# Linear attention with a one-token FFN on one core: kv sums in blocks of four token tiles, FFN batches of eight, part of wo on POOL's queue

## The chip, the cores and the metric

The kernel runs on one core of a Trainium2 chip. The metric is the device time of one execution in microseconds (us), the median over several executions. The profile covers a span that ends about 1.5 us short of that time. A run counts as fast unless it is over 1.5% above the fastest of the same kernel; every timed run told here is a fast one, except one single look whose state is not known.

## The reference, cut to what matters

```python
x = A_x                                              # 1 x 2048 x 1024, bf16
g = sigmoid((x * gate_w).sum(-1, keepdims=True))
# branch A: linear attention, 32 heads of 32, phi(t) = (t+1 if t>0 else exp(t)) + 1e-6
q, k, v = split(x @ wqkv)
kv = einsum("bhsd,bhse->bhde", phi(k), v);  z = phi(k).sum over s
o  = (phi(q) @ kv) / (phi(q) . z + 1e-6)
a  = o @ wo
# branch B: one FFN row, for the token with the largest x @ w_r, added at that row of x
y  = (silu(x_sel @ w_gate) * (x_sel @ w_up)) @ w_down * sigmoid(r_sel)     # F = 3584
b  = x with y added in that row
out = g * a + (1 - g) * b
```

## The kernel before

Names in the profile: `ps` is a buffer in PSUM, into which the program has TensorE write its results and out of which VectorE and ScalarE copy them ("evacuate" them); `pk` and `pq_all` are phi of k and q, `vt` is v, `kvacc` the kv sums, `wt` a streamed piece of weights, `h_bf` and `hps` h before and after its transposition, `yacc` and `yps` the down projection before and after its last sum, and `xp` a copy of x into which the chosen row, with y added, is written.

TensorE multiplies 16 token tiles by wk and wv (`unit_KV`, four units of eight 128x512 matmuls per tile), with units of q (`unit_Q`) between. Into this stream of full 128*128 matmuls two other kinds are mixed. The kv sums use 128*64 tiles:

```python
def unit_KVACC(t):
    for g in range(NG):
        for h in range(2):
            pe.matmul(kv_slot(g)[64 * h : 64 * h + 64, :], lhsT=pk_t[t][:, g * P + 64 * h : g * P + 64 * h + 64],
                      rhs=vt_t[t][:, g, h, :], start=False, stop=False, skip_group_check=True, tile_position=(0, 64 * h))
    # ... (the two buffers are given back)
```

The FFN of the one chosen row uses 128*32 tiles, four column tiles at a time; its weights stream through nine buffers, one piece after another:

```python
for j in range(4):        # compute() of one piece of gate_up
    pe.matmul(ps[32 * j : 32 * j + 32, 0:w], lhsT=xs_pad[:, c, :], rhs=wt[:, w * j : w * j + w],
                     start=(c == 0), stop=(c == KC - 1), tile_position=(0, 32 * j))
# ... after the last piece of up: h on VectorE, and h_transpose is left "pending" for ffn_flush()
```

The down projection is not on TensorE: VectorE adds each row of w_down, scaled by h, to `yacc`. What is mixed where is decided by tables and by this loop:

```python
GU_AFTER = {(6, "end"), (7, 1), (7, "end"), (8, 1), (8, "end"), (9, "end"), (10, "end"), (11, "end")}
# ...
def ffn_step(n):
    for _ in range(n):
        ffn_flush()
        wt, comp = inflight.popleft()
        comp(wt)
        ffn_prefetch()
# ...
for t in range(4, NT):
    for nb in range(4):
        unit_KV(t, nb)
        if nb == 1 and t > 4 and t % 2 == 0:
            unit_KVACC(t - 2)
            unit_KVACC(t - 1)
        if (t, nb) in GU_AFTER:
            ffn_step(4)
        steps = DOWN_STEPS.get(t, ())
        if nb < len(steps):
            down_step(steps[nb])          # also flushes first
    # ... units of q, FFN batches at the "end" of a token tile
```

After that come the denominators (`dps`), the product of kv with wo (`pm`), the rest of q, and 16 output tiles of 16 matmuls each.

## Time and profile before

| | before |
|---|---|
| time, median | 254.4 us (254.27 to 254.54, 3 runs) |
| span of the profile | 252.7 us |
| visits of 128*64 and 128*32 tiles from token tile 4 on | 6 kv blocks of 32 matmuls, 8 FFN batches of 16, one pair of them adjacent |
| last matmul start to end of the span | 248.59 to 252.72: 4.1 us |

How long SyncE (SP) closes the program shows in the view of the kernel's last line, restricted to SP. Columns: operation, count, duration ns min/median/max, first and last start us.

```profile
L702 SPq EVENT_SEMAPHORE  x12: 17/28/28, 249.9 to 252.7; - x12
L702 SPq DRAIN  x3: 7/7/128, 251.7 to 252.2; - x3
```

SyncE starts its closing checks (waits for the semaphores of queues and engines) at 249.9, and reaches its first drain at 251.7, 1.8 us on. The first drain takes 128 ns.

### The profile page before, as it was taken

The page shows a single profiled execution, that of the slowest core. Times are in us where ns is not written, and L with a number is a line of the kernel's source. Part 1 is how long each engine was busy: PE and PEld are TensorE (multiplying, and loading weights), DVE is VectorE, ACT ScalarE, POOL GpSimd, SP SyncE. Part 2 cuts the span into 40 slices and gives each one's busy share as a digit, 9 for nine tenths or more (in the row PEclk, how much of TensorE's full clock was granted, in tenths as well). Part 3 has the DMA queues.
Part 4 walks back from the last instruction along what each step waited for, and adds up shares of the span by engine and source line. Part 5 has one row for each costly group of instructions (what it writes and reads, how often), then busy time and mean ns, then how long its engine had stood idle before and what let it go on. Part 6 is the DMA issues. An engine that isn't in the chain of part 4 may idle for free.

```text
span 252.7 us, 4218 instructions
## 1 busy us (share of the span) xinstructions
PE 246.5 (98%) x1626; PEld 110.6 (44%) x1626; DVE 146.4 (58%) x240; ACT 125.4 (50%) x200; POOL 47.6 (19%) x94
## 2 busy tenths in 40 slices
PE   7999999999999999999999999999999999999993
PEld 2444454444444444444444444444444444444442
DVE  0045024324164369996899712585888999954442
ACT  2096334545354445555545635568888633333300
POOL 5000011010000000000000000210666689940000
PEclk9999999999999999999999999999999999999999
DMA  6999990029999989869896860030000573454122
GB/s 212 292 335 225 255 338 11 0 67 324 350 349 334 341 269 313 291 199 333 292 488 219 199 137 0 17 127 9 0 1 5 161 221 136 165 168 159 49 83 84
DMA packets 47499, 47.74 MB, mean 189 GB/s; under 512 B 18732, under 2 KB 35380, under 8 KB 47416
## 3 DMA queue, kind: packets, MB, share of 16 engines
q1 hardware_dynamic: 47192, 47.34, 61.5%
q8 instruction: 12, 0.20, 0.3%
q0 software_dynamic: 256, 0.14, 0.2%
q14 instruction: 7, 0.06, 0.1%
q10 hardware_dynamic: 32, 0.00, 0.0%
HBM read 39.34 MB, written 8.40 MB: 189 GB/s over the span
## 4 chain that ended last, share of the span: by engine, by line
PE 95%; DMA 2%; SPq 0%; DVE 0%; issue 0%; DVEq 0%
PE ps L78 88%; PE first L78 3%; PE kvacc L78 2%; DMA wkv<-in_A_wqkv_dram 2%; PE dps L78 1%; PE rps L78 1%; PE pm L78 1%; SPq L78 0%; DVE ot L78 0%; PE yps L78 0%; PE xs_ps L78 0%; DVEq L702 0%; PE pt L78 0%; PE hps L78 0%; PE wps L78 0%
## 5 line engine op out<-in xcount | busy, mean ns | idle before, releaser
L78 PE MATMUL ps<-wkv,xT 128*128 128x512 bf16 x480 | 107.3, 379 | 0.0
L78 PEld LDWEIGHTS <-xT 128*128 128x128 bf16 x512 | 48.6, 98 | 60.2 <-issue 3.7
L78 PE MATMUL ps<-xT,wq 128*128 128x512 bf16 x256 | 58.4, 379 | 0.0
L78 PE MATMUL ps<-m_sb,pq_all 128*128 128x512 bf16 (+2 forms) x264 | 55.6, 373 | 0.0
L78 ACT ACTIVATE u<-ps 128x512 f32<-128x512 f32 x60 | 35.8, 597 | 39.6 <-PE ps L78 38.0
L78 ACT ACTIVATE e<-u 128x512 f32<-128x512 f32 x64 | 40.3, 630 | 2.0
L605 POOL TENSOR_TENSOR pq_all<-pq_all,rb 128x512 bf16<-128x512 bf16 x32 | 36.6, 1168 | 14.4 <-DVE rb L78 13.9
L78 PEld LDWEIGHTS <-pq_all 128*128 128x128 bf16 x264 | 25.5, 98 | 30.2 <-issue 0.4
L78 PEld LDWEIGHTS <-wq 128*128 128x128 bf16 x256 | 24.5, 98 | 30.4 <-issue 1.7
L78 DVE SCALAR_TENSOR_TENSOR pq_all<-ps,e 128x512 bf16<-128x512 f32 x32 | 22.0, 688 | 26.2 <-ACT e L78 26.0
L78 DVE SCALAR_TENSOR_TENSOR yacc<-wt,hcol,yacc 128x1024 f32<-128x1024 bf16 x27 | 34.6, 1280 | 2.8 <-DMA wt<-in_B_w_down_dram 2.2
L78 ACT CAST vt<-ps 128x512 bf16<-128x512 f32 x32 | 18.8, 587 | 33.2 <-PE ps L78 33.2
L78 DVE SCALAR_TENSOR_TENSOR ot<-ps,gate,xg 128x512 bf16<-128x512 f32 (+2 forms) x33 | 23.8, 733 | 15.1 <-PE ps L78 14.2
L78 ACT ACTIVATE xg<-xt,omg 128x1024 f32<-128x1024 bf16 x16 | 18.1, 1145 | 25.9 <-DVE ot L78 25.9
L78 DVE SCALAR_TENSOR_TENSOR pk<-ps,e 128x512 bf16<-128x512 f32 x28 | 19.2, 686 | 18.3 <-ACT e L78 18.3
L78 DVE STREAM_SHUFFLE rb<-rdp 128x512 f32<-128x512 f32 x32 | 22.7, 742 | 0.0
L205 POOL MEMSET vt<- 128x16 bf16 x16 | 2.5, 191 | 105.5 <-PE kvacc L78 105.0
L78 DVE CAST r_bf<-rps 128x512 bf16<-128x512 f32 x1 | 0.7, 692 | 12.6 <-PE rps L78 12.6
L78 PE MATMUL first<-wkv,xT 128*128 128x512 bf16 x32 | 7.2, 379 | 0.7 <-DMA wkv<-in_A_wqkv_dram 0.6
L78 DVE SCALAR_TENSOR_TENSOR pk<-first,e 128x512 bf16<-128x512 f32 x4 | 2.8, 691 | 8.6 <-ACT e L78 8.6
L78 PE MATMUL ps<-wt,xs_pad 128*32 128x512 bf16 (+1 forms) x128 | 7.5, 355 | 0.0
L514 POOL DMA_DIRECT2D xp<-brow x1 | 0.6, 573 | 34.3 <-DVE zcol L78 34.3
(96 smaller groups left out, 82.7 us busy)
## 6 DMA issues: line engine op xcount, KB each, us to landing
wt<-in_B_w_down_dram SPq DMA_DIRECT2D x14, 512.0 KB, 6.2
wt<-in_B_w_gate_dram SPq DMA_DIRECT2D x8, 512.0 KB, 6.9
wt<-in_B_w_up_dram SPq DMA_DIRECT2D x8, 512.0 KB, 8.8
xt<-xp SPq DMA_DIRECT2D x16, 256.0 KB, 2.9
out_dram<-ot SPq DMA_DIRECT2D x15, 256.0 KB, 2.0
wt<-in_B_w_gate_dram SPq DMA_DIRECT2D x8, 384.0 KB, 5.9
wt<-in_B_w_up_dram SPq DMA_DIRECT2D x8, 384.0 KB, 6.9
wkv<-in_A_wqkv_dram SPq DMA_DIRECT2D x8, 256.0 KB, 5.1
```

The lines of the kernel that those rows point to most:

```text
L78: inst = fn(*a, **k)
L205: nc.gpsimd.memset(vt_t[t][:, :, :, 64:65], 1.0)
L514: nc.gpsimd.dma_start(out=xp[bass.ds(nonlocal_idx[0], 1), :].rearrange("o (j n) -> (o j) n", j=4), in_=brow[0:128:32, :])
L605: nc.gpsimd.tensor_tensor(sl, sl, rb[:], op=ALU.mult)
```

## The change

The intent is fewer changes of TensorE's tile shape: kv sums four token tiles at a time, the second FFN half in two batches of eight pieces, and two FFN batches placed right behind a kv block. The rest makes room for that: a fifth kv buffer, another order of weight pieces and down steps, transpositions of h at fixed later places in place of "before the next step", and eight of the 16 wo loads on POOL's queue.

```diff
-GU_AFTER = {(6, "end"), (7, 1), (7, "end"), (8, 1), (8, "end"), (9, "end"), (10, "end"), (11, "end")}
+GU_AFTER = {(6, "end"): 4, (7, 1): 4, (7, "end"): 4, (8, 1): 4, (10, 1): 8, (12, 1): 8}
+FLUSH_AFTER = {(8, 3), (13, 0)}
 ... (DOWN_STEPS: 28 steps as before, placed later)
-    kvp = ph1.enter_context(tc.tile_pool(name="kvp", bufs=4))
+    kvp = ph1.enter_context(tc.tile_pool(name="kvp", bufs=5))
 ... (wo_pieces)
-                    ld = nc.sync.dma_start(out=wt[32 * r : 32 * r + 32, :].rearrange("p (c n) -> p c n", c=2),
-                                           in_=wo_v[k // 2, r][:, 2 * (k % 2) : 2 * (k % 2) + 2, :])
+                    eng = nc.sync if r % 2 == 0 else nc.gpsimd
+                    ld = eng.dma_start(out=wt[32 * r : 32 * r + 32, :].rearrange("p (c n) -> p c n", c=2),
+                                       in_=wo_v[k // 2, r][:, 2 * (k % 2) : 2 * (k % 2) + 2, :])
 ... (ffn_pieces)
-        for _ in range(4):
-            yield from islice(gu, 4)
-            yield from islice(dn, 2)
+        for n in (2, 4):
+            yield from islice(dn, n)
+            yield from islice(gu, 8)
 ... (ffn_step, down_step)
-            ffn_flush()
 ... (token loop)
-            if nb == 1 and t > 4 and t % 2 == 0:
-                unit_KVACC(t - 2)
-                unit_KVACC(t - 1)
-            if (t, nb) in GU_AFTER:
-                ffn_step(4)
+            if nb == 1 and t > 4 and t % 4 == 0:
+                for t0 in range(t - 4, t):
+                    unit_KVACC(t0)
+            ffn_step(GU_AFTER.get((t, nb), 0))
+            if (t, nb) in FLUSH_AFTER:
+                ffn_flush()
 ...
-    unit_KVACC(NT - 2)
-    unit_KVACC(NT - 1)
+    for t in range(NT - 4, NT):
+        unit_KVACC(t)
```

More of the change, by code (lines that the diff above doesn't have):

```diff
@@ L33 @@
 Q_PER_T = {4: 2, 5: 1, 6: 1, 7: 2, 8: 1, 9: 1, 10: 2, 11: 1, 12: 1, 13: 1, 14: 1, 15: 0}
-GU_AFTER = {(6, "end"), (7, 1), (7, "end"), (8, 1), (8, "end"), (9, "end"), (10, "end"), (11, "end")}
+GU_AFTER = {(6, "end"): 4, (7, 1): 4, (7, "end"): 4, (8, 1): 4, (10, 1): 8, (12, 1): 8}
+FLUSH_AFTER = {(8, 3), (13, 0)}
 M_AFTER = {3: (0, 0), 6: (0, 1), 9: (1, 0), 12: (1, 1)}
-DOWN_STEPS = {9: (1, 1, 1, 1), 10: (1, 1, 1, 1), 11: (1, 1, 1, 1), 12: (1, 1, 1, 1, 1), 13: (1, 1, 1, 1), 14: (1, 1, 1, 1), 15: (1, 1, 1)}
+DOWN_STEPS = {9: (1, 1, 1, 1), 10: (0, 0, 1, 1, 1, 1), 11: (1, 1, 1, 1), 12: (0, 0, 1, 1, 1), 13: (1, 1, 1, 1, 1), 14: (1, 1, 1, 1, 1), 15: (1, 1, 1)}
 FFN_DEPTH = 9
@@ L496, in down_step @@
         for _ in range(n):
-            ffn_flush()
             if down["cur"] is None:
@@ L539 @@
             router_part2()
-        if (t, "end") in GU_AFTER:
-            ffn_step(4)
+        ffn_step(GU_AFTER.get((t, "end"), 0))
     unit_Q(*q_units.popleft())
-    unit_KVACC(NT - 2)
-    unit_KVACC(NT - 1)
+    for t in range(NT - 4, NT):
+        unit_KVACC(t)
     down_finish()
```

## The prediction

> **What bounds the kernel now.** I began with the page: busy shares first, then the chain that ended last.
>
> ```profile
> PE 246.5 (98%) x1626; PEld 110.6 (44%) x1626; DVE 146.4 (58%) x240; ACT 125.4 (50%) x200; POOL 47.6 (19%) x94
> ...
> PE 95%; DMA 2%; SPq 0%; DVE 0%; issue 0%; DVEq 0%
> ```
>
> TensorE (PE) is busy 98% of the span and is 95% of the chain, so only PE time moves the end. A busy PE need not be an efficient PE: matmul ends are modelled, so I read starts. Next I took the timeline of PE in the stretch where the attention stream (128*128 tiles) is interrupted by the FFN (128*32 tiles) and by the kv sums (128*64 tiles). Columns: start us, length, engine, line, operation, out<-in, tile, shape, count.
>
> ```profile
> 60.54 0.70 PE L78 MATMUL kvacc<-vt,pk 128*64 128x65 bf16 x32
> 61.17 3.63 PE L78 MATMUL ps<-wkv,xT 128*128 128x512 bf16 x16
> 64.63 1.89 PE L78 MATMUL ps<-xT,wq 128*128 128x512 bf16 x8
> 66.45 1.05 PE L78 MATMUL ps<-wt,xs_pad 128*32 128x512 bf16 x16
> 67.43 3.63 PE L78 MATMUL ps<-wkv,xT 128*128 128x512 bf16 x16
> 70.99 1.05 PE L78 MATMUL ps<-wt,xs_pad 128*32 128x512 bf16 x16
> 71.97 3.63 PE L78 MATMUL ps<-wkv,xT 128*128 128x512 bf16 x16
> 75.43 3.62 PE L78 MATMUL ps<-xT,wq 128*128 128x512 bf16 x16
> ```
>
> Read start to start. From 61.17 to 64.63, with no border behind them, 16 matmuls take 3.46 us, 0.216 each. The 16 from 67.43 to 70.99, with a border behind, take 3.56 us, 0.10 more. No wait shows there; PE never sits idle for a releaser in this stretch. The extra lies at the borders. Between single starts in the trace the last 128*128 matmul before a border is 0.309 us from its successor (0.093 too much), the last 128*32 one is 0.312 us from its successor (0.096 too much), and the first matmul after each border takes 0.227 (0.011 too much). These are costs of changing tile shape, and PE being "busy" hides them.
>
> Third, the chain in order of time shows what a kv block costs by its length:
>
> ```profile
> 36.50 1.14 PE kvacc L78 x64
> ...
> 60.61 0.63 PE kvacc L78 x32
> ```
>
> Another 32 matmuls cost 1.14 - 0.63 = 0.51 us, 16 ns each, so a block of 32 holds 0.63 - 0.51 = 0.12 us that does not depend on its length.
>
> **What the Trainium skill says.** "TensorEngine Tiling (Array Packing)", Key Properties: "Changing tiling mode (not just tile) drains the TensorE". The trace agrees; it puts about 0.10 us on each border. "TensorE: Matmul & The Clock Gate", Back-to-back issue gap, gives N/2.4 + 2.5 ns for a warm matmul: 216 ns at 512 columns, 162.5 at 384; the trace shows 216, and 162 between groups of four of 384 columns. It says four column tiles run together (Part 3); here four start within 10 ns of each other. "DMA: Bandwidth & Descriptors", Issuing engines are not separate DMA queues, says that spreading issues over engines saves only sequencer time. I rest on that for the wo part; no row here tests it.
>
> **The change part by part.** An excursion is a departure from the 128*128 stream and the return.
> - kv block, fixed cost: entry 0.093, inside 0.12, first matmul after it 0.011: 0.223 us.
> - FFN batch of 16 matmuls at 512 columns: 0.98 us first start to first start after it; its four groups at 0.216 make 0.864, leaving 0.116; with 0.093 and 0.011, 0.220 us.
>
> *kv sums in fours.* From token tile 4 on there are six blocks of 32 now and three of 64 after. The matmuls are the same, three excursions go: 3 x 0.223 = 0.67 us.
>
> *Second FFN half in two batches.* Four batches of 16 become two of 32: 2 x 0.220 = 0.44 us. Gate and up keep their eight groups of four.
>
> *FFN right behind kv blocks.* Now one FFN batch follows a kv block directly (84.15); after, two do (token tiles 8 and 12). The build order confirms both. In the trace of before the 128*64 to 128*32 border costs as much as the return to full tiles would (kv block 0.630 us against 0.631, FFN batch 0.98 either way), so adjacency only drops one departure from 128*128 and one first matmul: 0.093 + 0.011 = 0.10 us for the one added pair.
>
> *Half of wo on POOL's queue.* Eight of 16 wo issues leave SyncE. Those issues were 124.8 to 147.6 us, most of it behind the copy into xp; wo is first used at 171.5. Worth 0. POOL's vt memsets all precede these DMAs in its program order, so none is held up behind a wo wait. The fifth kvp buffer is needed because four tiles wait while a fifth is filled.
>
> Sum: 0.67 + 0.44 + 0.10 = 1.21 us on PE, all on the path, as there is no other wait to fill. 254.4 - 1.2 = 253.2.
>
> **The rivals.**
>
> *A. VectorE makes PE wait.* PSUM has four work banks, so each Q or kv unit (1.73 us) must be evacuated before the fourth one behind it starts. VectorE does part of that in program order, with the down projection (yacc) between. Already now it is tight:
>
> ```profile
> 97.26 5.23 DVE L78 SCALAR_TENSOR_TENSOR yacc<-wt,hcol,yacc 128x1024 f32<-128x1024 bf16 x4
> 102.42 0.68 DVE L78 SCALAR_TENSOR_TENSOR pq_all<-ps,e 128x512 bf16<-128x512 f32 x1
> 103.02 0.35 DVE L78 TENSOR_SCALAR eg<-eg 128x384 f32<-128x384 f32 x1
> 103.40 2.55 DVE L78 RECIPROCAL eg<-eg 128x384 f32<-128x384 f32 x1
> ...
> 112.63 1.44 DVE L78 SCALAR_TENSOR_TENSOR pq_all<-ps,e 128x512 bf16<-128x512 f32 x2
> 116.32 1.28 DVE L78 SCALAR_TENSOR_TENSOR yacc<-wt,hcol,yacc 128x1024 f32<-128x1024 bf16 x1 [2.25 <-DMA wt<-in_B_w_down_dram]
> ```
>
> I walked the changed order on VectorE with steps from this trace: yacc to yacc 1.32 us start to start, yacc to an evacuation 1.20, evacuation to yacc 0.60, reciprocal 2.47; an evacuation is ready 1.46 us after its unit's last slot (unit ended at 69.2, pk evacuated from 70.66). By my count the gate batch of 32 starts at about 102.4 and ends at 103.8, with Q units ending at 109.0 and 110.7. The down tile whose first half is queued between the two pk evacuations of token tile 10 can only be loaded after the tile before it is consumed (100.2, since eight buffers hold gate weights); issue to landing of a lone one is about 3.5 us (issued 112.74, used 116.32), so 103.75. Then yacc 103.75, pk 104.95, yacc 105.55, eg 106.75, yacc 107.1, reciprocal 108.3, yacc 110.8, sg 112.0, pq 112.5 to 113.15. The bank that pq frees is wanted at 114.2: 1.0 us of room. The next two have about 0.9 each. In tiles 13 to 15 the same walk leaves 1.3 us or more. So: no stall, but little room. If that load took 5 us instead of 3.5, some 0.5 us of PE time would be lost and the result 253.7; a loss over 1.2 us needs a load of nearly 6 us.
>
> *B. Weights late for a batch of eight.* A batch needs eight tiles resident out of nine buffers. The eighth gate tile is issued when the first down tile is consumed, about 91.0, and lands by 95, against 102.4. The eighth up tile is issued about 112, wanted at 124. Room of 7 us and more. If it failed, each late tile would stop PE by its lateness; I give it little.
>
> *C. The borders are hidden anyway, or longer visits cost more.* Against: the kv block of 64 already in the trace shows no extra cost, and starts, not modelled ends, carry the numbers. If half of the border cost came back elsewhere, 253.8.
>
> *D. The copy into xp comes later.* It is issued at 123.5 now, about 127 after, behind six down tiles, and landed in 16.4 us; so about 144 to 146. The selected row is written into xp at 161, and wo is used at 171. Hidden.
>
> **Range and chances.** Central 253.2; runs of one kernel spread 0.27 us. Rival A or C skews the range up: 252.9 to 253.9. The whole gain is 0.5%, and 2% is 5 us: no removed cost sums to that and no stall found is nearly as long. Faster by over 2%: 0.01; within 2%: 0.98; slower: 0.01.
>
> **What would show it.** Nine visits (three kv, six FFN) with two adjacent pairs, so seven departures from 128*128 in place of 13, in the PE timeline from 60 to 160 us; kv blocks of 64 at 1.14 us; FFN batches of 32 at 1.42 us (0.77 + 4 x 0.162); the yps matmuls starting 1.2 us earlier than 159.06, and the same distance from there to the end. Wrong would be: PE idle before a ps group released by VectorE near 110 to 118 us (rival A), or by a wt DMA at about 102 or 124 (B), or the gain of yps lost again after 160 (D).

## The result, and the profile after

| | before | after |
|---|---|---|
| time, median of 4 runs of the same rounds | 254.47 us (254.27 to 254.81) | 252.54 us (252.19 to 252.62) |
| ratio of the means of fast runs | | 0.992 (95% interval 0.9903 to 0.9937) |
| the profiled run: time, span | 254.26, 252.72 us | 252.49, 250.95 us |

A ratio is the mean time of one kernel's fast runs over that of the other's in the same rounds, so not quite the ratio of the medians. The gain is 1.93 us by the medians and 1.77 us between the two profiled executions, against 1.21 predicted; 252.54 lies below the range of 252.9 to 253.9. I had been wrong about the size.

The page of the kernel after, busy shares and chain:

```profile
PE 244.2 (97%) x1601; PEld 111.7 (45%) x1626; DVE 145.9 (58%) x240; ACT 125.6 (50%) x200; POOL 51.8 (21%) x102
...
PE 95%; DMA 2%; issue 1%; SPq 0%; DVE 0%; DVEq 0%
```

TensorE still carries 95% of the chain. The 2.3 us between its busy times must not be read as the gain: this trace has 1601 matmul records where 1626 were executed (1626 weight loads are there), so 25 are lost. Only starts are safe. The timeline of PE after, in the same stretch as in the prediction and at the other merged places:

```profile
59.72 4.26 PE L79 MATMUL ps<-wkv,xT 128*128 128x512 bf16 x19
63.82 1.89 PE L79 MATMUL ps<-xT,wq 128*128 128x512 bf16 x8
65.64 1.05 PE L79 MATMUL ps<-wt,xs_pad 128*32 128x512 bf16 x16
66.62 3.63 PE L79 MATMUL ps<-wkv,xT 128*128 128x512 bf16 x15
...
82.70 1.21 PE L79 MATMUL kvacc<-vt,pk 128*64 128x65 bf16 x64
83.84 1.05 PE L79 MATMUL ps<-wt,xs_pad 128*32 128x512 bf16 x16
```

The kv block at 60.5 is gone; the stream runs unbroken from kv units into q units. The block of token tiles 4 to 7 takes 83.84 - 82.70 = 1.14 us, and the FFN batch follows it directly. Farther on, from the same view of the kernel after:

```profile
102.29 1.48 PE L79 MATMUL ps<-wt,xs_pad 128*32 128x384 bf16 x32
103.71 3.63 PE L79 MATMUL ps<-wkv,xT 128*128 128x512 bf16 x15
...
122.81 1.21 PE L79 MATMUL kvacc<-vt,pk 128*64 128x65 bf16 x64
123.95 1.48 PE L79 MATMUL ps<-wt,xs_pad 128*32 128x384 bf16 x32
```

A merged FFN batch takes 103.71 - 102.29 = 1.42 us, as predicted. To weigh the whole loop without the start-up, I use two fixed points, the first kv matmul and the first denominator matmul: 36.43 and 163.19 before, 36.36 and 161.89 after. The timeline of PE before has them as

```profile
36.43 1.21 PE L78 MATMUL kvacc<-vt,pk 128*64 128x65 bf16 x64
...
163.19 1.05 PE L78 MATMUL dps<-pq_all,zc 128*32 128x512 bf16 x16
```

and after they are

```profile
36.36 1.21 PE L79 MATMUL kvacc<-vt,pk 128*64 128x65 bf16 x64
...
161.89 1.05 PE L79 MATMUL dps<-pq_all,zc 128*32 128x512 bf16 x16
```

So this interval, called "the loop" from here on, fell from 126.76 to 125.53 us: 1.23 us. From the first denominator matmul of the second group to the last matmul both kernels take the same 52.75 us. What else changed lies behind the last matmul, which (by the single starts in the traces) begins at 248.59 before and 247.29 after: the rest to the end fell from 4.12 to 3.66 us. The closing lines of SP in the kernel after:

```profile
L702 SPq EVENT_SEMAPHORE  x12: 17/28/28, 248.6 to 250.9; - x12
L702 SPq DRAIN  x3: 7/7/13, 250.1 to 250.4; - x3
```

From the first closing check to the first drain it is now 1.5 us, not 1.8, and the drain takes 13 ns, not 128. So the account of the profiled pair is 1.23 us of loop, 0.46 of closing stretch, 0.07 of start-up (first kv matmul at 36.36, not 36.43), together 1.76 of the 1.77 us.

My theory after this: the borders cost what I said, and SyncE's program ends sooner because it has eight DMA issues fewer. The rival: all 1.93 us are borders, dearer than I counted, and the closing stretch is chance of one profile.

### The profile page after: what moved, and what is told of

The parts are those of the page before. It is cut to its first block, busy times and chain, and to the rows that moved or that the text cites. A ratio compares the mean times of both kernels' runs of the same rounds, so it can differ in the third digit from the quotient of the medians.

```text
span 251.0 us, 4198 instructions
## 1 busy us (share of the span) xinstructions
PE 244.2 (97%) x1601; PEld 111.7 (45%) x1626; DVE 145.9 (58%) x240; ACT 125.6 (50%) x200; POOL 51.8 (21%) x102
## 4 chain that ended last, share of the span: by engine, by line
PE 95%; DMA 2%; issue 1%; SPq 0%; DVE 0%; DVEq 0%
PE ps L79 88%; PE first L79 3%; DMA wkv<-in_A_wqkv_dram 2%; PE kvacc L79 2%; PE dps L79 1%; PE rps L79 1%; PE pm L79 1%; SPq L79 0%; DVE ot L79 0%; PE yps L79 0%; PE xs_ps L79 0%; DVEq L702 0%; PE pt L79 0%; PE hps L79 0%; PE wps L79 0%
## 5 line engine op out<-in xcount | busy, mean ns | idle before, releaser
L79 PE MATMUL ps<-wkv,xT 128*128 128x512 bf16 x468 | 106.1, 379 | 0.6
L79 PEld LDWEIGHTS <-xT 128*128 128x128 bf16 x512 | 49.2, 98 | 60.7 <-issue 3.0
L79 PE MATMUL ps<-xT,wq 128*128 128x512 bf16 x249 | 57.5, 379 | 0.7 <-issue 0.5
L79 DVE SCALAR_TENSOR_TENSOR pk<-ps,e 128x512 bf16<-128x512 f32 x28 | 19.2, 688 | 16.4 <-ACT e L79 16.4
L79 DVE RECIPROCAL rd<-dn 128x512 f32<-128x512 f32 x2 | 6.7, 3346 | 0.0
```

Of the source, the lines that this page charges most:

```text
L79: inst = fn(*a, **k)
```

## The experiments

All twelve runs gave correct results. Three groups shared chip and rounds, and the last ran alone; times of different groups are not compared with each other except through the kernel before (254.04, 254.34, 254.02 and 254.08 us in the four, in the order of the table). "The loop" and "the close" (last matmul start to end of span) are from each run's profile.

| run | loop us | close us | SP instructions recorded | time us | ratio to before (95%) |
|---|---|---|---|---|---|
| before | 126.76 | 4.12 | 212 | 254.47 | |
| after | 125.53 | 3.66 | 206 | 252.54 | 0.992 (0.9903 to 0.9937) |
| a_wosync | 125.53 | 4.03 | 214 | 252.76 | 0.9935 (0.9906 to 0.9964) |
| b_wohalf | 126.76 | 3.65 | 204 | 253.69 | 0.9969 (0.994 to 0.9999) |
| b_kv4 | 126.15 | 4.12 | 212 | 253.41 | 0.997 (0.9939 to 1.0) |
| b_gu8 | 127.55 | 4.02 | 215 | 254.75 | 1.0012 (0.9981 to 1.0043) |
| after_again | 125.54 | 3.66 | 206 | 252.59 | 0.9925 (0.9885 to 0.9964) |
| a_split | 125.53 | 4.03 | 214 | 252.83 | 0.9932 (0.9887 to 0.9978) |
| b_gu8flush | 126.32 | 4.02 | 214 | 253.5 | 0.9965 (0.9929 to 1.0001) |
| a_noadj | 125.64 | 3.66 | 206 | 252.64 | 0.9917 (0.9871 to 0.9964) |
| a_first8 | 126.44 | 3.66 | 206 | 253.52 | 0.9984 (0.9956 to 1.0013) |
| a_first8late | 125.20 | 3.66 | 207 | 251.8 | 0.9932 (0.9897 to 0.9968) |
| b_wo4 | 126.75 | 3.43 | 208 | 253.35 (one run) | |
| a_first8late2 | 125.20 | 3.66 | 207 | 252.61 | 0.9924 (0.9906 to 0.9941) |

Times scatter by some tenths of a us within a kernel, and single executions by more (the kernel before took 253.32 to 256.46 in one group). Part of it is start-up: the first kv matmul came between 35.68 and 38.25 us in these profiles. The loop and the close repeat to 0.01 us. The loop is a difference of two starts that are rounded to 0.01 us; from the unrounded starts the four loops of 125.53 and 125.54 are all 125.54, and the fall from before is 1.22.

**a_wosync: the kernel after, all of wo back on SyncE.**

```diff
-                    eng = nc.sync if r % 2 == 0 else nc.gpsimd
+                    eng = nc.sync
```

> The changed kernel with all 16 wo issues back on SyncE. Theory (tile-shape borders give 1.2 us; about 0.4 us more comes from SyncE closing the program sooner, 250.02 to 250.15 after the last queue check against 251.34 to 251.92 before, because it has 8 issues fewer): TensorE starts as in the changed kernel, closing stretch 0.4 us longer, time about 252.95. Rival (all 1.93 us are borders, the closing stretch is chance of one profile): 252.5.

The loop stayed at 125.53 and the close grew to 4.03. The wo part does nothing to TensorE and 0.37 us to the close. The theory holds.

**b_wohalf: the kernel before, with only the wo part.**

```diff
-                    ld = nc.sync.dma_start(
+                    eng = nc.sync if r % 2 == 0 else nc.gpsimd
+                    ld = eng.dma_start(
```

> The kernel before with only the wo part of the change. Theory: TensorE unmoved to 0.1 us, closing stretch 0.4 us shorter, 254.05. Rival: 254.45, nothing.

The loop is 126.76, as before; the close 3.65. In time, 253.69 against 254.04 in the same rounds: a part that I had priced at 0 is worth 0.47 us of closing.

**b_kv4: the kernel before, with only kv sums in fours.**

```diff
-    kvp = ph1.enter_context(tc.tile_pool(name="kvp", bufs=4))
+    kvp = ph1.enter_context(tc.tile_pool(name="kvp", bufs=5))
-            if nb == 1 and t > 4 and t % 2 == 0:
-                unit_KVACC(t - 2)
-                unit_KVACC(t - 1)
+            if nb == 1 and t > 4 and t % 4 == 0:
+                for t0 in range(t - 4, t):
+                    unit_KVACC(t0)
 ... (and the last four tiles behind the loop)
```

> The kernel before with only kv sums in fours (and the fifth buffer). Theory: 3 x 0.223 = 0.67 us off TensorE's path, 253.8. In it the FFN batch at token tile 8 stays adjacent, the others are apart. Rival (borders dearer than counted, 1.93 in place of 1.21 in all): 253.4.

The loop fell by 0.61, not 0.67 and not 1.07. The missing 0.06 is visible: the last matmul in front of the second transposition of h (hps) is 0.278 us from it, against 0.216 in an unbroken stream, and hps starts 0.057 us after h_bf ends, where in the kernel before h had been ready for 1.01 us. So the three kv excursions cost 0.67 as counted, and hps waited a little for h.

**b_gu8: the kernel before, with only the second half in two batches of eight.**

```diff
-GU_AFTER = {..., (8, "end"), (9, "end"), (10, "end"), (11, "end")}
+GU_AFTER = {..., (9, "end"): 8, (11, "end"): 8}
 ... (ffn_pieces as in the change; ffn_flush() stays inside ffn_step and down_step)
```

> The kernel before with only the second FFN half in two batches of eight, placed at ends of token tiles 9 and 11, away from kv blocks. Theory: 2 x 0.220 = 0.44 us off TensorE, 254.0, with the closing stretch as before or unknown (SyncE has three semaphore waits more). Rival (borders dearer): 253.75.

A miss: the loop grew to 127.55. The timeline of PE in this run:

```profile
121.63 1.90 PE L78 MATMUL ps<-wkv,xT 128*128 128x512 bf16 x8
124.59 0.23 PE L78 MATMUL hps<-sel,h_bf 128*128 128x4 bf16 x3 [1.06 <-DVE h_bf L78]
```

TensorE sat idle until VectorE had made h. The eight matmuls in front should have taken 1.73 us and hps began 2.96 us after their start, so 1.23 us were lost; 0.44 gained and 1.23 lost are the 0.79 measured. The timeline of VectorE (DVE) in this run tells why h was late:

```profile
120.86 2.61 DVE L78 SCALAR_TENSOR_TENSOR yacc<-wt,hcol,yacc 128x1024 f32<-128x1024 bf16 x2 [2.29 <-DMA wt<-in_B_w_down_dram]
123.38 0.68 DVE L78 SCALAR_TENSOR_TENSOR pq_all<-ps,e 128x512 bf16<-128x512 f32 x1
123.98 0.55 DVE L78 TENSOR_TENSOR h_bf<-ps,sg 128x384 bf16<-128x384 f32 x1
```

h stands in VectorE's program order behind two down steps, which had waited 2.29 us for their weights. So the transposition of h cannot stay where it was. The change moves it (the flush table), and I had read that part only as bookkeeping.

**b_gu8flush: the same with the transposition of h at a later fixed place.**

```diff
 def ffn_step(n): / def down_step(n):
-            ffn_flush()
 ... (token loop, behind the FFN step)
+            if (t, nb) in {(8, 3), (12, 3)}:
+                ffn_flush()
```

> The two-batch run again, with the transposition of h moved three token units later, as the change does too. Theory (in the first such run a gain of 0.44 was eaten by one wait of 1.2 us of TensorE for h on VectorE, which stood behind yacc instructions): the wait goes, first kv to first denominator matmul 126.76 - 0.44 = 126.32, where the first run had 127.55. Rival (two batches of eight cost something else besides): stays above 126.8.

The loop is 126.32, to the hundredth what two excursions of 0.22 us make it. So batches of eight are worth 0.44, but only with the later transposition, which alone is worth 1.23 here (127.55 - 126.32).

**a_noadj: the kernel after, with one adjacency undone.**

```diff
-GU_AFTER = {..., (10, 1): 8, (12, 1): 8}
+GU_AFTER = {..., (10, 1): 8, (11, "end"): 8}
```

> The changed kernel with its last FFN batch at the end of token tile 11 in place of right behind the kv block of tile 12, so one adjacency less. Theory: one more departure, 0.10 us: first kv to first denominator matmul 125.63 against 125.53. Rival (adjacency saves a whole excursion, 0.22): 125.75; (saves nothing): 125.53.

The loop is 125.64, 0.10 to 0.11 more than 125.53 and 125.54. An adjacency is worth one departure, not an excursion.

**after_again: the kernel after, unaltered, beside other runs.** No edit.

> The changed kernel unaltered, on the chip of the runs beside it. Theory (borders 1.23 us of TensorE time, and a pause of 0.4 us in SyncE's closing checks that the kernel before has and this one has not): first kv matmul to first denominator matmul 125.53 us again (126.76 before), last matmul to end 3.66 again (4.12 before), ratio to before about 0.9935. Rival (the closing stretch is chance): it comes out near 4.1 this time, or varies.

Loop and close repeat to 0.01 us. The rival that the close is chance falls.

**a_split: the kernel after, with SyncE's wo loads cut in two each.** POOL still issues its half, but SyncE has eight more issues.

```diff
-                    ld = eng.dma_start(out=wt[32 * r : 32 * r + 32, :]. ..., in_=wo_v[k // 2, r][:, 2 * (k % 2) : 2 * (k % 2) + 2, :])
+                    for c in ((0, 1) if r % 2 == 0 else ((0, 2),)):
+                        ... one dma_start for c, or one for both
```

> The changed kernel with SyncE's eight wo loads cut in two each, so that SyncE has 216 instructions again though POOL still issues half of wo. Theory (the pause falls where SyncE reaches the 208th recorded instruction of its program, whatever the instructions are): pause back, last matmul to end about 4.0, as with all wo on SyncE; TensorE as in the changed kernel. Rival (the use of POOL's queue shortens the close): 3.66.

The close is 4.03 again:

```profile
L704 SPq EVENT_SEMAPHORE  x12: 17/28/28, 248.4 to 251.0; - x12
L704 SPq DRAIN  x3: 7/7/13, 250.2 to 250.5; - x3
```

It is not POOL's queue that shortens it; it is the number of instructions on SyncE. The starts of SP's last instructions in the traces say more. In each kernel with a long close there is one pause of some 0.39 us between two closing instructions that otherwise follow each other within 0.1. In the kernel before and in b_kv4 it lies in front of the fifth from last of 212; in a_wosync, a_split and b_gu8flush in front of the seventh from last of 214; in b_gu8 in front of the eighth from last of 215. That is the 208th recorded instruction each time (212 - 4 = 214 - 6 = 215 - 7 = 208). The kernels with 204 to 207 have no such pause.

**b_wo4: the kernel before, with four wo loads on POOL.**

```diff
+                    eng = nc.sync if r < 3 else nc.gpsimd
```

> The kernel before with only four wo issues moved to POOL, so SyncE has 208 recorded instructions in place of 212. Theory (pause before the 208th recorded one): the pause falls on the very last, which waits for the other engines about 0.49 us anyway, so it is hidden: last matmul to end about 3.66 with TensorE as before (126.76). Rival (the pause is at a fixed distance from the end): 4.1.

No pause shows: SP's last instruction, the 208th, comes 0.49 us behind the one before it, as in the other kernels, because it waits for the other engines. A pause at a fixed distance from the end is out. But the close was 3.43, shorter than I expected. The checks stand in a fixed order of semaphores, and here the last output transfer was checked later in the row, so fewer checks of 0.06 us were left once it had landed.

**a_first8: the kernel after, with the first FFN half in batches of eight too.**

```diff
-GU_AFTER = {(6, "end"): 4, (7, 1): 4, (7, "end"): 4, (8, 1): 4, (10, 1): 8, (12, 1): 8}
+GU_AFTER = {(7, 1): 8, (8, 1): 8, (10, 1): 8, (12, 1): 8}
```

> The changed kernel with its first FFN half, too, in two batches of eight: behind the second kv unit of token tiles 7 and 8, the latter right behind the kv block. Theory: two excursions fewer, 2 x 0.22 = 0.44 us, first kv to first denominator matmul 125.53 - 0.44 = 125.09, time about 252.1, if eight up tiles are there by 83.4; seven of them are issued only as the gate batch ends near 71.5, and 3.5 MB at the 350 GB/s of those slices take 10 us after some 2 us, so about 83.5. Rival: the last tiles are late and TensorE waits up to 1 us, a loss.

The rival came true, and VectorE added to the loss. The timeline of PE in this run:

```profile
82.22 1.69 PE L79 MATMUL ps<-wt,xs_pad 128*32 128x512 bf16 x28
84.55 0.40 PE L79 MATMUL ps<-wt,xs_pad 128*32 128x512 bf16 x4 [0.64 <-DMA wt<-in_B_w_up_dram]
...
114.53 3.68 PE L79 MATMUL ps<-wkv,xT 128*128 128x512 bf16 x16 [0.23 <-DVE pq_all L79]
```

The eighth up tile was late. The up batch took 2.67 us from its start to the next stream matmul, where the gate batch took 1.84: 0.83 us lost. And near 114 TensorE waited for VectorE: the 32 kv matmuls from 110.69 on took 7.43 us where 6.91 is usual, 0.52 lost. 125.54 - 0.44 + 0.83 + 0.52 = 126.45, measured 126.44.

**a_first8late: the same with the up batch two kv units later.**

```diff
-GU_AFTER = {(6, "end"): 4, (7, 1): 4, (7, "end"): 4, (8, 1): 4, (10, 1): 8, (12, 1): 8}
-FLUSH_AFTER = {(8, 3), (13, 0)}
+GU_AFTER = {(7, 1): 8, (8, 3): 8, (10, 1): 8, (12, 1): 8}
+FLUSH_AFTER = {(9, 1), (13, 0)}
-DOWN_STEPS = {9: (1, 1, 1, 1), ...
+DOWN_STEPS = {9: (0, 1, 1, 2), ...
```

> As the run beside it, but the up batch two kv units later (end of token tile 8), not adjacent to the kv block, and the down projection starts one unit later. Theory: no DMA wait; 0.44 gained, 0.10 of adjacency given back, 125.53 - 0.34 = 125.19. Rival: VectorE, with the down work squeezed, makes TensorE wait, above 125.5.

The loop is 125.20, where 125.19 was expected. It beats both kernels on TensorE's path, by 0.34 us over the kernel after. One of its six runs took 253.94, so I ran it again. (The record places that excess outside the program's span: the span of this run was 250.6 us, those of the others 249.8 to 251.0.)

> The fastest version so far once more, since its first timing had one run at 253.9 among runs near 251.7. Theory (0.34 us less TensorE time than the changed kernel, the same short close): 125.20 from first kv to first denominator matmul again, ratio to before near 0.991 where the changed kernel had 0.992 and 0.9925. Rival (the down work squeezed into fewer slots stalls TensorE in some executions, which the one slow run would have shown): the interval longer than 125.3 or a ratio over 0.9935.

The loop is 125.20 again although this execution was slow (254.05; its first kv matmul came at 38.25 instead of about 36, at start-up). TensorE does not stall in the loop. The ratio, 0.9924, cannot be told from that of the kernel after; 0.34 us is less than the scatter of start-up. So the better loop is shown, a better time is not.

## Why the prediction was right or wrong

**The borders: right, to 0.02 us.** Predicted 1.21, measured 1.23 in the loop. Term by term: kv sums in fours 0.67 (0.61 alone, plus 0.06 that hps waited), batches of eight 0.44 (126.76 - 126.32), the added adjacency 0.10 (0.10 to 0.11 in a_noadj). The three sum as if they did not touch each other. So reading starts rather than busy time, and taking the cost of a border from the gaps in front of and behind it, was sound.

**Rival A (VectorE): right, and closer than its name suggests.** The walk through VectorE's order had pq at 112.5 to 113.15. The timeline of VectorE in the kernel after:

```profile
104.02 1.28 DVE L79 SCALAR_TENSOR_TENSOR yacc<-wt,hcol,yacc 128x1024 f32<-128x1024 bf16 x1 [1.36 <-DMA wt<-in_B_w_down_dram]
105.22 0.68 DVE L79 SCALAR_TENSOR_TENSOR pk<-ps,e 128x512 bf16<-128x512 f32 x1
...
112.51 0.68 DVE L79 SCALAR_TENSOR_TENSOR pq_all<-ps,e 128x512 bf16<-128x512 f32 x1
```

The down tile was waited for, as expected, and pq stands at 112.51. In the kernel after TensorE does not wait; in a_first8, where the same pq came at 113.80, 1.29 us later, it did, and lost 0.52. Its kv units began 0.06 later there (110.69, not 110.63), so the room in the kernel after was about 1.29 - 0.06 - 0.52 = 0.7 us, where I had counted 1.0: room there was, but less. What the prediction missed of VectorE is the other queue position: h for the transposition. b_gu8 shows that, at its places, the two batches without the moved flush cost 0.79 us instead of gaining 0.44. I counted the flush as neither gain nor risk; it is a condition of the gain. That the change came with it, and so met no such wait, is luck as far as the prediction goes.

**Rivals B, C and D: did not happen.** No weights were late in the kernel after, the borders came off in full, and the copy into xp stayed hidden, though it landed later than I said: it was issued at 128.6 and took 23.9 us, so 152.5, where I had 144 to 146 (and my own numbers, 127 and 16.4, add up to 143.4); the selected row is written into xp at 159.9.

**The step that failed: "Worth 0" for half of wo, and with it "only PE time moves the end".** The chain said 95% TensorE and I treated the rest as fixed. It is not: behind the last matmul SyncE closes the program, and what was on SyncE's list decides how long that takes. Taking eight issues off it removed a pause worth 0.47 us in the kernel before (b_wohalf) and 0.37 in the kernel after (a_wosync). One of my own signs failed by it: the yps matmuls came 1.30 us earlier (157.76, not 159.06; 0.07 of it start-up), but their distance to the end, which I had called unchanged, fell from 93.66 to 93.19 us. In the profiled pair the close fell by 0.46. With that the account is 1.23 + 0.46 = 1.69, and 254.47 - 1.69 = 252.78 would have fallen a little below my range, too. The other 0.24 us up to the 1.93 between medians is start-up (0.07 in the profiled pair) and scatter of runs (the profiled run of before was 0.21 below its median, that of after 0.05, a net 0.16); I can't attribute it further.

**The range** leaned to slow results, because every rival I had thought of was a loss. That is a second mistake: I asked what could go wrong with each moved piece, and not what else a moved piece might free.

**What stays open:** why SyncE pauses at its 208th instruction. In all fourteen profiles the pause is paid where SyncE has 212 recorded instructions or more and not seen where it has 208 or fewer. In the trace of before, the instruction transfers nearest to the pause (251.34 to 251.73) start at 219.7 and 252.4, so none runs during it. But the later one keeps step with the 208th instruction: in all six profiles with the long close a transfer of 8 KB on the instruction queue starts 0.62 to 0.64 us after that instruction does (0.53 in b_wo4), while in the seven with 204 to 207 the last such transfer starts 1.0 us or more after SyncE's last instruction has ended. So the supply of instructions is the rival to look at first. No run tested it.

## What to carry to other kernels

Count how often a matmul stream changes tile shape, price each border from start-to-start gaps (about 0.1 us a border, 0.22 an excursion here), and merge visits, but look in the order of the other engines for each small result that a merged visit delays. Look at the close of the program too: here one engine closes for all, and eight issues moved off its list were worth 0.37 to 0.47 us, though their own work was hidden. That rests on where its list ends: between 215 and 212 recorded instructions the close changed by 0.1 us, and at 208 or fewer no pause showed. That this change fell on the good side was luck. And if a part of a change looks worthless, measure it alone before it is written off.

## What the Trainium skill lacked or had wrong

- "TensorEngine Tiling (Array Packing)", Key Properties, says that a change of mode drains TensorE but gives no cost. Here: 0.093 to 0.096 us in front of a border, 0.011 in the first matmul behind it, about 0.22 us for an excursion from 128*128 and back; from 128*64 straight to 128*32 costs as much as the return to full tiles would, and an adjacency saves 0.10.
- "TensorE: Matmul & The Clock Gate", Back-to-back issue gap, gives about 131 ns per matmul at 512 columns as the sustained rate of weight loads and matmuls, and says that N/2.4 + 2.5 over-counts there. Here the formula holds: 216 ns in every long stretch of such pairs.
- "DMA: Bandwidth & Descriptors", Issuing engines are not separate DMA queues, says that spreading issues saves only sequencer time. The loop agrees (126.76 with and without it), but the close does not: eight issues fewer on SyncE were worth 0.37 to 0.47 us of the whole, not as time to issue them but because the shorter list has no pause among the closing checks.
- No page that I used mentions the pause of about 0.39 us in front of the 208th recorded instruction of SyncE's program, or that the order of the closing checks shifts the end (close of 3.43 us against 3.66).
